# Products on zeros in TensorE's early waits, and a register list laid out in pieces of 64 bytes, in a windowed-attention and mixture-of-experts kernel

## Chip, cores, metric

One core of a Trainium2 chip. The metric is the device time of one execution in microseconds (us): the median of three runs of the kernel before is 216.32 us, from 215.83 to 216.89.

## What is computed

The input is q, k and v of 8 batches, 8 heads, 576 positions and 64 channels. Every position attends to the positions at most 32 away. The result, 4608 tokens of 512 channels, goes through a mixture of eight experts in which each token uses the one with the largest logit.

```python
scores = scale * np.matmul(q, k.transpose(0, 1, 3, 2))
mask = np.abs(pos[:, None] - pos[None, :]) <= window        # window = 32
attn = softmax(np.where(mask, scores, -1e9))
x = np.matmul(attn, v)        # as (N, D) = (4608, 512)
logits = x @ w_gate + modality_bias[modality_id]
e_idx = np.argmax(logits, axis=1)
for e in range(8):
    mask = e_idx == e
    h = np.maximum(x[mask] @ w1[e], 0.0)
    out[mask] = gate_w[mask, None] * (h @ w2[e])
```

## The kernel before

The modality bias of these inputs is large, so all tokens of one modality go to one expert. The kernel sorts the tokens by modality into one transposed list XT, with the tokens of modality 0 from the left and the others from the right, and multiplies each side by the weights of its one expert. A check of all this at the end leads to a general branch if it does not hold.

**The order is written out by hand.** The string ORDER names every piece of work in the order in which it is recorded. A piece is a name, numbers, an engine after a slash, and the PSUM banks after a colon. Each engine runs its own pieces in this order and waits where an input is not there. So a piece that waits holds back what stands behind it on its engine, and nothing on the others. The pieces that matter here:

- `l` loads q and k of a batch (line 211, issued by GpSimd), `t` transposes them on VectorE (line 651). `lv` loads v, `W` loads an expert's weights.
- `MA` and `MB` write the band mask into PSUM as products of `ident` and `neg` (lines 660, 664). `SA` and `SB` are the scores of one group of four heads (line 683), `sa` and `sb` their exponentials on ScalarE (lines 691, 694).
- `V` multiplies with v (line 725), `v` divides by the row sums on VectorE (lines 737, 738) into `xt`. `M` masks on VectorE (line 708), in all heads whose mask was not put into PSUM.
- `s` works out each token's place in the list: `s0` on ScalarE (line 163), `s1`, `s4`, `s5`, `s7` on TensorE, and `s9` writes the place of each of the 40 blocks of tokens as an integer to `off_i` (line 476 ff.).
- `r0` to `r3` load these places, ten at a time, into registers of ScalarE (line 768), which uses them as addresses in `pa` and `pb`, the copies of a block to the list (lines 779, 793). `X` makes a block's columns (line 759).
- `Je` and `Jo` make one-hot tables on VectorE and GpSimd (lines 503, 519, 522, 525), from which `Jm` (line 533) makes the list of output rows.
- `U` is the product with w1 (line 897), `u` its ReLU (line 914), `D` the product with w2 (line 923), `y` the scaling and `O` the scattered store (line 942).

A list of ten places is 40 bytes, and the four lists lie behind one another in `off_i`, so that they begin at byte 0, 40, 80 and 120:

```python
off_i = const.tile([P, NC], I32)
_, rs_ = nc.values_load_multi_w_load_instructions(
    off_i[0:1, n_ * i:n_ * i + n_], engines=[ET.Activation], min_val=0, max_val=N,
```

A piece `n` (function `idle`, line 949) exists in the code, but ORDER does not use it: it writes products that nobody reads into a bank.

Of the kernel before, what the change touches and what calls it, by code (L numbers as in the profile page):

```python
# [31 lines left out]


ORDER = """
Km Kw0/v l0.1.0/p l0.0.0/p Kp0/a Kj/p l0.1.1/p e0/v e1/v Kp1/v Kn0/p Kq1/v Kq0/v l0.0.1/p MA0.0:0123 Ke/v Kw2/v l1.0.2/p
Kh/v t0.0.1/v Ki Kw1/p Kn1/p e2/v e3/v e4/v t0.0.0/v Kg lv0.0/p Ko1/v t0.1.1/v SA0.0 Kc5/p MA0.1:4567 sa0.0/a t0.1.0/v
Kc1/p Kv/p lv0.1/p SA0.1 Kc3/p MB0.0:0123 sa0.1/a t1.1.0/v l1.1.2/p SB0.0 W1.0/p Ko0/v s0/a t1.0.0/v MB0.1:4567 sb0.0/a
SB0.1 Kc2/p sb0.1/a s1:0 Kc0/p V0:12 s2/v s3/v Kc4/p s4 s5 v0/v lv1.0/p Kb/a V2:34 s6/v s8/v s11/v e6/v V1:12 v2/v s12/p
s7 V3:56 e7/p Kc6/p v1/v s9/a s10/a r0/a W1.1/p t1.0.1/v r1/a lv1.1/p v3/v SA1.0:0123 W2.0/p s13/v t1.1.1/v SB1.0:4567
sa1.0/a l2.0.2/p s15/v Ko2/v e8/v s14/v s17/v sb1.0/a G0/v SB1.1:0123 s16/v c0/v Je1.0/v Je0.0/v Jy2/v Je0.1/p sb1.1/a  # L40
X0.0:5 M5/v X0.4:4 l2.1.2/p X0.1:7 Je0.2/p Jy10/v Jo1/v l3.1.2/p pb0.0/a X0.2:2 M4/v pa0.0/a V5:01 pb0.1/a e5/p l3.0.2/p
X0.3:5 pa0.1/a v5/v pb0.2/a Je1.1/p V4:67 pa0.2/a pb0.3/a Jo0/v Je1.2/p pa0.3/a SA1.1:0123 lv2.0/p v4/v pb0.4/a pa0.4/a
Jm0:5 G1/v sa1.1/a Kc7/p U0.1:4 Jo2/v U0.0:6 Je2.0/v u0.1/a M7/v U1.3:0 Je2.1/p Je3.0/v W2.1/p U1.0:7 M6/v u1.3/a u0.0/a
e9/p V7:12 Je3.1/v u1.0/a Je2.2/v U0.2:6 v7/v lv2.1/p V6:34 u0.2/a U0.3:0 r2/a Je3.2/p v6/v U1.2:1 Jo3/v u0.3/a L0:7
X1.2:0 X1.0:6 lo0/v Jx0/v Jm1:3 pa1.0/a X1.1:7 D0.1.0:4 Je5.0/v pb1.0/a Jx1/v Jo5/v Je5.1/p pb1.1/a D0.0.0:6 E0/a
pa1.1/a sm0/v Je4.0/v pb1.2/a rc0/v G2/v Je4.1/p X1.3:3 pa1.2/a X1.4:7 D0.0.1 pa1.3/a t2.0.0/v pa1.4/a D0.1.1 pb1.3/a
Jo4/v pb1.4/a U2.3:0 y0.1/a Je5.2/v Je4.2/v t2.0.1/v L1:3 u1.2/a Jm2:7 y0.0/a U3.2:5 lo1/v u2.3/a s19/v Jo6/v SB2.0:1234
Je7.0/v U2.2:0 Je7.1/v sb2.0/a Je7.2/v Jx2/v U2.1:6 t2.1.1/v U2.0:7 t2.1.0/v u2.1/a u2.2/a SA2.0:1234 Jo7/v u2.0/a
U3.3:6 E1/a sa2.0/a Je6.0/v U3.1:7 t3.0.1/v Je6.1/p U1.1:0 Je6.2/p u3.1/a M9/v l4.0.2/p u3.3/a SA2.1:1234 u1.1/a M8/v
lv3.0/p D2.0.0:7 sa2.1/a Jm3:0 D2.0.1 l4.1.2/p Jx3/v sm1/v u3.2/a Jy1/v lv3.1/p Jy3/v SB2.1:0123 Jy0/v Jy4/v t3.0.0/v  # L50
D2.1.0:6 sb2.1/a Jy5/v V9:45 rc1/v D2.1.1 v9/v y2.0/a V8:01 M10/v y2.1/a SB3.0:2345 U3.0:6 v8/v sb3.0/a D1.1.0:7 M11/v
V10:01 r3/a Jy8/v Jy6/v V11:45 v10/v D1.1.1 u3.0/a v11/v D1.0.0:0 y1.1/a Jy7/v X2.0:2 Jy9/v X2.1:3 G3/v X2.2:7 O0.1/p
pa2.0/a D3.1.0:1 pb2.0/a t4.1.0/v pa2.1/a X2.3:6 pb2.1/a O0.0/p D3.0.0:2 pa2.2/a t4.0.0/v pb2.2/a D1.0.1 pa2.3/a pb2.3/a
X2.4:7 D3.0.1 y1.0/v pb2.4/a pa2.4/a t3.1.1/v O1.0/p D3.1.1 SA3.0:4567 t3.1.0/v O2.0/p U5.0:0 sa3.0/a t4.1.1/v U4.2:3
y3.0/v u5.0/a SB3.1:4567 u4.2/v O3.0/p U5.2:2 sb3.1/a M12/v U4.3:3 O1.1/p M13/v U5.1:0 y3.1/a l5.1.2/p t4.0.1/v V12:45
u5.1/a O2.1/p U5.3:1 u5.2/a v12/v u4.3/a L2:0 l5.0.2/p V13:67 lo2/v SA3.1:2345 E2/a lv4.1/p v13/v U4.0:0 sa3.1/a u5.3/v
l6.1.2/p U4.1:6 u4.0/a D5.0.0:1 M14/v u4.1/a SB4.0:2345 sm2/v c1/v M15/v D4.0.0:0 sb4.0/a V14:67 c2/v rc2/v D5.0.1 v14/v
V15:23 y5.0/a c3/v SA4.1:4567 v15/v O5.0/p D4.0.1 sa4.1/a t5.1.1/v X3.0:2 D4.1.0:1 lv5.0/p pa3.0/a y4.0/v X3.1:5 pb3.0/a
X3.4:3 X3.2:6 pa3.1/a t5.1.0/v lv4.0/p D4.1.1 pb3.1/a pa3.2/a X3.3:0 t5.0.0/v pb3.2/a D5.1.0:2 pa3.3/a pb3.3/a
# [1165 lines left out]
```

## Time and profile before

| | |
|---|---|
| median of three runs | 216.32 us (215.83 to 216.89) |
| the profiled execution | 216.04 us |
| its span, first to last instruction | 214.4 us |
| mean granted TensorE clock of the span | 0.962 |
| busy: TensorE, VectorE, ScalarE, GpSimd | 189.3, 151.5, 133.8, 99.0 us |
| q, k, v and weights moved by GpSimd's DMA queue | 27.79 MB with the stores |

In the rows below PE is TensorE, PEld its weight load, DVE VectorE, ACT ScalarE, POOL GpSimd. A letter q behind an engine is its sequencer. L12 is line 12 of the kernel. Times are us from the start of the span unless marked ns.

### The profile page before, as it was taken

The numbers are of one execution on the slowest core, as the hardware profiler recorded it, in microseconds if no ns is written. First come the engines' busy times: TensorE is split into PE (matmuls) and PEld (weight loads), VectorE is DVE, ScalarE is ACT, GpSimd is POOL, SyncE is SP. The second block draws the span as 40 slices with busy tenths as digits, with TensorE's granted clock in tenths as the row PEclk, the third lists the DMA queues.
The fourth block names the chain that finished last, engine by engine and source line by source line (L and its number), as shares of the span: only waits on it lengthen the run. The fifth ranks groups of instructions, "written<-read, shape, count | busy, mean of one in ns | idle before, by whom it ended". The sixth has DMA issues, their size and how long they took to land.

```text
span 214.4 us, 6043 instructions
## 1 busy us (share of the span) xinstructions
PE 189.3 (88%) x2474; PEld 135.7 (63%) x2497; DVE 151.5 (71%) x300; ACT 133.8 (62%) x224; POOL 99.0 (46%) x138
## 2 busy tenths in 40 slices
PE   0578469999999989999999999999999999999940
PEld 0246368868766568558875786686597668566610
DVE  3865989899889896899899588977377527311610
ACT  5149397588976468697688679859974622244110
POOL 7886779950710656168640673240070322025350
PEclk9999758999999999999999999999999999999995
DMA  4999999999999349999999799224030121113211
GB/s 73 172 173 203 194 206 198 211 214 192 192 189 140 145 151 180 193 186 175 222 187 96 252 158 158 101 98 189 12 121 32 50 101 49 49 52 147 98 63 47
DMA packets 47629, 30.39 MB, mean 142 GB/s; under 512 B 38852, under 2 KB 38892, under 8 KB 47340
## 3 DMA queue, kind: packets, MB, share of 16 engines
q0 software_dynamic: 46576, 27.79, 82.0%
q1 hardware_dynamic: 1019, 2.16, 2.9%
q8 instruction: 21, 0.34, 0.7%
...
HBM read 36.76 MB, written 9.70 MB: 217 GB/s over the span
## 4 chain that ended last, share of the span: by engine, by line
PE 76%; POOL 7%; DVE 5%; DMA 3%; issue 3%; ACT 2%; another core or an unknown queue 1%; POOLq 0%; DVEq 0%
PE banks L923 29%; PE banks L897 26%; PE banks L683 7%; PE banks L725 7%; PE banks L759 3%; DMA qk<-in_q_dram 3%; POOL qk L211 2%; PE banks L824 2%; DVE qk L651 2%; ACT pt L691 1%; POOL ev L525 1%; PE banks L660 1%; DVE xt L738 1%; POOL ev L522 1%
## 5 line engine op out<-in xcount | busy, mean ns | idle before, releaser
L942 POOL DMA_INDIRECT out_dram<-ys,ids x37 | 42.0, 1136 | 91.8 <-ACT ys L933 39.9
L897 PE MATMUL banks<-XT,w_sb 128*128 128x256 bf16 x576 | 70.3, 273 | 0.3 <-DVE xt L738 0.3
L923 PE MATMUL banks<-w_sb,hT 128*128 128x512 bf16 x265 | 67.7, 379 | 1.2
L897 PEld LDWEIGHTS <-w_sb 128*128 128x128 bf16 x576 | 54.3, 98 | 11.8 <-issue 1.6
L691 ACT ACTIVATE pt<-banks 128x1536 bf16<-128x1536 f32 x32 | 46.4, 1452 | 24.3 <-PE banks L683 17.9
L914 ACT ACTIVATE hT<-banks 128x512 bf16<-128x512 f32 x56 | 31.7, 599 | 21.2 <-PE banks L897 20.8
L923 PEld LDWEIGHTS <-hT 128*128 128x128 bf16 x296 | 26.6, 98 | 24.3 <-issue 0.6
L651 DVE STREAM_TRANSPOSE qk<-qk 128x576 int32<-128x576 int32 x32 | 38.7, 1248 | 3.5 <-DMA qk<-in_q_dram 2.0
L708 DVE TENSOR_TENSOR pt<-pt,mask 128x1920 bf16<-128x1920 bf16 x28 | 32.1, 1166 | 6.1 <-ACT pt L691 4.6
L683 PE MATMUL banks<-qk 32*128 32x192 bf16 (+1 forms) x640 | 20.9, 260 | 7.2 <-DVE qk L651 3.5
L738 DVE TENSOR_TENSOR xt<-banks,recs 128x640 bf16<-128x640 f32 x32 | 26.4, 825 | 1.1
L912 DVE TENSOR_SCALAR hT<-banks 128x512 bf16<-128x512 f32 x18 | 12.4, 688 | 18.3 <-PE banks L897 18.2
L725 PE MATMUL banks<-vt,pt 128*128 128x65 bf16 x576 | 23.9, 196 | 1.6 <-ACT pt L694 1.2
L725 PEld LDWEIGHTS <-pt 128*128 128x128 bf16 x576 | 22.1, 100 | 4.2 <-issue 1.2
L683 PEld LDWEIGHTS <-qk 32*128 32x128 bf16 x640 | 14.2, 100 | 15.2 <-issue 9.6
L933 ACT ACTIVATE ys<-banks,Gt 128x512 f32<-128x512 f32 x20 | 13.6, 691 | 11.6 <-PE banks L923 11.5
L779 ACT CAST XT<-banks 128x352 f32 (+3 forms) x40 | 18.0, 451 | 3.8 <-PE banks L759 3.2
L227 POOL DMA_DIRECT2D vt<-in_v_dram x16 | 20.3, 1274 | 0.0
L793 ACT CAST XT<-banks 128x352 f32 (+2 forms) x39 | 17.6, 451 | 3.3 <-PE banks L759 2.6
L935 DVE TENSOR_SCALAR ys<-banks,Gt 128x512 f32<-128x512 f32 x17 | 12.5, 735 | 7.8 <-PE banks L923 4.9
L759 PE MATMUL banks<-oh,xt 128*128 128x128 bf16 (+1 forms) x160 | 13.1, 224 | 1.4 <-ACT pt L694 1.4
L759 PEld LDWEIGHTS <-xt 128*128 128x128 bf16 x160 | 10.7, 103 | 4.8 <-issue 1.5
...
## 6 DMA issues: line engine op xcount, KB each, us to landing
vt<-in_v_dram POOLq DMA_DIRECT2D x16, 288.0 KB
...
qk<-in_q_dram POOLq DMA_DIRECT2D x7, 576.0 KB
qk<-in_k_dram POOLq DMA_DIRECT2D x7, 576.0 KB
...
out_dram<-ys,ids POOLq DMA_INDIRECT x37
qk<-in_k_dram POOLq DMA_DIRECT2D x2, 288.0 KB
qk<-in_q_dram POOLq DMA_DIRECT2D x2, 288.0 KB
```

What stands on the lines that cost most here:

```text
L227: nc.gpsimd.dma_start(v_t[b % NV][:, n_ * i:n_ * i + n_, 0:D], v[b].rearrange("h s d -> (h s) d").rearrange("(n p) d -> p n d", p=P)[:, n_ ...
L651: nc.vector.transpose(qk_t[b % 2][:, g, at:at + S].rearrange("p (t r) -> p r t", r=R), Ct["l", b][:, u, g].bitcast(I32).rearrange("p (r j) ...
L683: nc.tensor.matmul(st[:, h, WIN * i_:WIN * i_ + w_], qk[32 * h:32 * h + 32, c_, QK + k0:QK + k0 + P], qk[32 * h:32 * h + 32, c_, q0:q0 + w ...
L691: nc.scalar.activation(pt[:, :, 2 * part:2 * part + 2, 0:WIN], st[:, :, 0:2 * WIN].rearrange("p h (j c) -> p h j c", c=WIN), ACT.Exp, scal ...
L708: nc.vector.tensor_tensor(out=p_ap, in0=p_ap, in1=mask[:], op=ALU.mult)
L725: nc.tensor.matmul(o_ap, pt[:, c1:c1 + P], vt[:, g0 + j, 0:D + 1], start=(m == 0 and i_ == 0), stop=(i_ == len(mine) - 1), skip_group_chec ...
L738: nc.vector.tensor_tensor(out=x_t[b % NX][:, :, P * hp:P * hp + P].rearrange("p m (h d) -> p h m d", h=2), in0=o_v[:, :, :, 0:D], in1=rec. ...
L759: nc.tensor.matmul(t_[:, kd, :], x_t[b % NX][:, m, P * kd:P * kd + P], Ct["oh", b][:, m, 0:n_], start=True, stop=True, skip_group_check=True)
L897: ins = nc.tensor.matmul(ph[:, u_, :], w1[:, f0:f0 + 2 * P - 1:2], rhs, start=(kd == 0), stop=(kd == n_kd - 1))
L914: nc.scalar.activation(o_ap, i_ap, ACT.Relu)
L923: nc.tensor.matmul(Ct["D", t_, s_], Ct["h", t_][:, kf, P * s_:P * s_ + P], w2, start=(kf == 0), stop=(kf == n_kf - 1))
L942: ins = nc.gpsimd.indirect_dma_start(out=out, out_offset=bass.IndirectOffsetOnAxis(ap=ids[:, u_:u_ + 1], axis=0), in_=Ct["y", t_, s_][:], ...
```

## The change

ORDER gets 24 pieces `n`, of four or two products of 256 columns each, 64 products in all. Their weights and their data are `zero_b`, a tile of zeros (the weights were `ident` in the unused function). Some names of other pieces change places in the string, but on every engine the other instructions stand in the order in which they stood. `off_i` gets 16 places for each list of ten, so that the lists begin at byte 0, 64, 128 and 192.

```diff
 ORDER = """
-Km Kw0/v l0.1.0/p l0.0.0/p Kp0/a Kj/p l0.1.1/p e0/v e1/v Kp1/v Kn0/p Kq1/v Kq0/v l0.0.1/p MA0.0:0123 Ke/v Kw2/v l1.0.2/p
+Km Kw0/v n4.256:0 l0.1.0/p l0.0.0/p n4.256:0 Kp0/a Kj/p n4.256:0 l0.1.1/p e0/v e1/v n4.256:0 Kp1/v Kn0/p Kq1/v n4.256:0
...
-    off_i = const.tile([P, NC], I32)
+    off_i = const.tile([P, B // RB, 16], I32)
...
-            copy(eng, off_i[:], Ct["off"][:, 0:NC])
+            copy(eng, off_i[:, :, 0:RB * NM], Ct["off"][:, 0:NC].rearrange("p (a c) -> p a c", c=RB * NM))
...
-            off_i[0:1, n_ * i:n_ * i + n_], engines=[ET.Activation], min_val=0, max_val=N,
+            off_i[0:1, i, 0:n_], engines=[ET.Activation], min_val=0, max_val=N,
...
-            nc.tensor.matmul(banks[:, bk[0], 0:w_], ident[:], zero_b[:, 0:w_], start=True, stop=True, skip_group_check=True)
+            nc.tensor.matmul(banks[:, bk[0], 0:w_], zero_b[:, 0:P], zero_b[:, 0:w_], start=True, stop=True, skip_group_check=True)
```

**First place: TensorE from its first instruction to the first scores.** Before, the mask products MA0.0 come first and the scores SA0.0 right behind them:

```order
L660 LDWEIGHTS ident [waits Pool_49]
L660 MATMUL banks<-neg,ident 128x384 [waits Pool_49]
...
L660 LDWEIGHTS ident
L660 MATMUL banks<-neg,ident 128x384
L683 LDWEIGHTS qk_84 [waits DVE_49]
L683 MATMUL banks<-qk_84 128x192 [waits DVE_49]
```

Now 28 products on zeros stand ahead of MA0.0, and 18 between MA0.0 and SA0.0:

```order
L953 LDWEIGHTS zero_b [waits DVE_49]
L953 MATMUL banks<-zero_b 128x256
...
L662 LDWEIGHTS ident [waits Pool_49]
L662 MATMUL banks<-neg,ident 128x384 [waits Pool_49]
...
L953 LDWEIGHTS zero_b
L953 MATMUL banks<-zero_b 128x256
...
L685 LDWEIGHTS qk_84 [waits DVE_49]
L685 MATMUL banks<-qk_84 128x192 [waits DVE_49]
```

The first of them wait for VectorE's memset of `zero_b` alone; the scores still wait for VectorE's transposes.

**Second place: TensorE behind SB0.1**, where the transpose s1 (line 459, now 461), the products V0, s4 and s5 (lines 467 and 470, now 469 and 472) and V2 follow. Before:

```order
L459 LDWEIGHTS midr [waits Activation_49]
L459 MATMUL banks<-ident,midr 128x40 [waits Activation_49]
L725 LDWEIGHTS pt_86 [waits DMASW5_49]
...
L467 LDWEIGHTS Am [waits DVE_49]
L467 MATMUL banks<-ones,Am 40x128
L470 LDWEIGHTS tri [waits Pool_49]
```

Now:

```order
L953 LDWEIGHTS zero_b
L953 MATMUL banks<-zero_b 128x256 [waits Activation_49]
...
L461 LDWEIGHTS midr
L461 MATMUL banks<-ident,midr 128x40
L727 LDWEIGHTS pt_86 [waits DMASW5_49]
...
L472 LDWEIGHTS tri [waits Pool_49]
L472 MATMUL banks<-Am,tri 128x40
L953 LDWEIGHTS zero_b
L953 MATMUL banks<-zero_b 128x256
...
L727 MATMUL banks<-vt_88,pt_87 128x65 [waits DMASW6_49]
```

Two products stand ahead of s1 and carry its wait for ScalarE's sb0.0 (both use bank 0); six stand between s5 and V2.

**Third place: TensorE between V3 and SA1.0.** Before, the scores of batch 1 followed V3 at once. Now ten products stand there, which wait first for VectorE (v2, bank 3) and then for ScalarE (s9 and s10, bank 0):

```order
L727 MATMUL banks<-vt_88,pt_87 128x65
L953 LDWEIGHTS zero_b
L953 MATMUL banks<-zero_b 128x256
...
L953 MATMUL banks<-zero_b 128x256 [waits DVE_49]
...
L953 MATMUL banks<-zero_b 128x256 [waits Activation_49]
...
L685 LDWEIGHTS qk_85 [waits DVE_49]
L685 MATMUL banks<-qk_85 128x192
```

Nothing on the other engines waits for a product on zeros, and behind SA1.0 TensorE's order has none.

## Rows read from the trace of the kernel before

**Rows 1.** Busy time in stretches; columns as in the first line

```profile
core 0: us, PE busy (x) PEld busy (x) DVE busy (x) ACT busy (x) POOL busy (x), PEclk, DMA share, GB/s
0.00:17.08 17.08, 8.51 (x77) 4.36 (x78) 10.36 (x32) 7.12 (x7) 13.86 (x45) 1.00 1.20 141
17.08:23.91 6.83, 4.25 (x105) 3.44 (x103) 5.09 (x14) 4.75 (x9) 4.34 (x12) 1.00 1.16 212
23.91:34.15 10.24, 7.58 (x136) 6.63 (x136) 8.93 (x23) 8.46 (x15) 8.32 (x11) 0.50 1.60 192
41.50:205.00 163.50, 160.85 (x2060) 114.66 (x2082) 119.30 (x217) 108.34 (x187) 63.65 (x60) 1.00 0.79 137
```

**Rows 2.** Chain that ended last, 12 to 21 us: start, us, what

```profile
12.23 0.83 PE banks L683 x15
13.06 1.39 PE banks L660 x4
14.45 0.43 PE banks L664 x4
14.88 0.97 PE banks L683 x24
...
17.23 0.22 PE banks L664 x4
17.45 0.60 PE banks L683 x20
...
18.07 1.45 ACT pt L691
19.52 0.49 ACT pt L694
...
20.07 0.53 PE banks L725 x11
```

**Rows 3.** Timeline of VectorE: start, us, engine, line, what, idle before

```profile
1.04 0.17 DVE L316 MEMSET zero_b<- 128x128 uint32 x1 [1.04 <-PEq L1209]
...
13.96 2.50 DVE L651 STREAM_TRANSPOSE qk<-qk 128x576 int32<-128x576 int32 x2 [1.78 <-DMA qk<-in_q_dram]
...
22.67 1.25 DVE L651 STREAM_TRANSPOSE qk<-qk 128x576 int32<-128x576 int32 x1
```

**Rows 4.** Timeline of TensorE: first scores, first product with w1

```profile
8.87 0.83 PE L683 MATMUL banks<-qk 32*128 32x192 bf16 x16 [2.39 <-DVE qk L651]
...
34.73 1.47 PE L897 MATMUL banks<-XT,w_sb 128*128 128x256 bf16 x12
```

**Rows 5.** Timeline of ScalarE

```profile
14.46 0.29 ACT L163 CAST midr<-mid 40x128 bf16<-40x128 int32 x1
...
21.78 0.19 ACT L163 CAST off_i<-banks 128x40 int32<-128x40 f32 x1
...
25.58 2.79 ACT L691 ACTIVATE pt<-banks 128x1536 bf16<-128x1536 f32 x2 [3.52 <-DVE posi L487]
...
34.45 1.45 ACT L691 ACTIVATE pt<-banks 128x1536 bf16<-128x1536 f32 x1 [0.19 <-PE banks L683]
```

**Rows 6.** Register loads, line 768: ns min/median/max; r0, r1, then r2 with r3

```profile
L768 ACTq TENSOR_LOAD <-off_i x1: 1193/1193/1193, 22.0 to 22.0; - x1
L768 ACTq TENSOR_LOAD <-off_i x1: 2173/2173/2173, 23.3 to 23.3; - x1
L768 ACTq TENSOR_LOAD <-off_i x2: 997/1596/2194, 39.9 to 63.7; - x2
```

**Rows 7.** The page's DMA issues: what, engine, count, KB each

```profile
vt<-in_v_dram POOLq DMA_DIRECT2D x16, 288.0 KB
...
qk<-in_k_dram POOLq DMA_DIRECT2D x7, 576.0 KB
```

**Rows 8.** Timeline of GpSimd

```profile
29.14 1.87 POOL L525 TENSOR_SCALAR ev<-ev,pr 128x180 bf16<-128x180 bf16 x1
...
33.56 0.96 POOL L525 TENSOR_SCALAR ev<-ev,pr 128x180 bf16<-128x180 bf16 x1
```

More of the change, by code (lines that the diff above doesn't have):

```diff
@@ L34 @@
 ORDER = """
-Km Kw0/v l0.1.0/p l0.0.0/p Kp0/a Kj/p l0.1.1/p e0/v e1/v Kp1/v Kn0/p Kq1/v Kq0/v l0.0.1/p MA0.0:0123 Ke/v Kw2/v l1.0.2/p
[L36 to L54, printed above, removed]
@@ L55 @@
-y3.0/v u5.0/a SB3.1:4567 u4.2/v O3.0/p U5.2:2 sb3.1/a M12/v U4.3:3 O1.1/p M13/v U5.1:0 y3.1/a l5.1.2/p t4.0.1/v V12:45
-u5.1/a O2.1/p U5.3:1 u5.2/a v12/v u4.3/a L2:0 l5.0.2/p V13:67 lo2/v SA3.1:2345 E2/a lv4.1/p v13/v U4.0:0 sa3.1/a u5.3/v
+Km Kw0/v n4.256:0 l0.1.0/p l0.0.0/p n4.256:0 Kp0/a Kj/p n4.256:0 l0.1.1/p e0/v e1/v n4.256:0 Kp1/v Kn0/p Kq1/v n4.256:0
+Kq0/v l0.0.1/p Ke/v n4.256:0 Kw2/v l1.0.2/p Kh/v t0.0.1/v Ki n4.256:0 Kw1/p Kn1/p MA0.0:0123 e2/v e3/v n4.256:4 e4/v
+t0.0.0/v n2.256:4 Kg n2.256:4 n2.256:4 lv0.0/p n2.256:4 Ko1/v n2.256:4 t0.1.1/v n2.256:4 n2.256:4 SA0.0 Kc5/p MA0.1:4567
@@ new lines @@
+sa0.0/a t0.1.0/v Kc1/p Kv/p lv0.1/p SA0.1 MB0.0:0123 Kc3/p sa0.1/a t1.1.0/v SB0.0 l1.1.2/p s0/a W1.0/p Ko0/v t1.0.0/v
+MB0.1:4567 sb0.0/a Kc2/p SB0.1 Kc0/p n2.256:0 s1:0 sb0.1/a V0:12 Kc4/p s2/v s3/v s4 s5 n2.256:3 v0/v n2.256:3 lv1.0/p
+n2.256:3 s6/v Kb/a s8/v V2:34 s11/v e6/v s12/p V1:12 e7/p v2/v Kc6/p s7 V3:56 n2.256:7 v1/v W1.1/p n2.256:3 s9/a s10/a
+n2.256:4 r0/a n2.256:0 n2.256:0 t1.0.1/v lv1.1/p r1/a v3/v SA1.0:0123 W2.0/p s13/v sa1.0/a t1.1.1/v SB1.0:4567 l2.0.2/p
+s15/v Ko2/v sb1.0/a e8/v SB1.1:0123 s14/v s17/v G0/v s16/v c0/v Je1.0/v Je0.0/v sb1.1/a X0.0:5 Jy2/v M5/v Je0.1/p X0.4:4
@@ new lines @@
+X0.1:7 l2.1.2/p Jy10/v Jo1/v Je0.2/p pb0.0/a X0.2:2 pa0.0/a l3.1.2/p M4/v V5:01 pb0.1/a pa0.1/a e5/p l3.0.2/p pb0.2/a
+X0.3:5 pa0.2/a v5/v V4:67 Je1.1/p pb0.3/a pa0.3/a Je1.2/p Jo0/v pb0.4/a SA1.1:0123 lv2.0/p pa0.4/a v4/v Jm0:5 sa1.1/a
+U0.1:4 G1/v Kc7/p Jo2/v U0.0:6 u0.1/a Je2.0/v U1.3:0 M7/v Je2.1/p U1.0:7 Je3.0/v u1.3/a W2.1/p M6/v u0.0/a V7:12 e9/p
+u1.0/a U0.2:6 Je3.1/v Je2.2/v v7/v lv2.1/p V6:34 u0.2/a U0.3:0 r2/a v6/v Je3.2/p U1.2:1 u0.3/a Jo3/v L0:7 X1.2:0 X1.0:6
+lo0/v Jx0/v Jm1:3 pa1.0/a X1.1:7 D0.1.0:4 Je5.0/v pb1.0/a Jx1/v Jo5/v Je5.1/p pb1.1/a D0.0.0:6 E0/a pa1.1/a sm0/v
@@ new lines @@
+Je4.0/v pb1.2/a rc0/v G2/v Je4.1/p X1.3:3 pa1.2/a X1.4:7 D0.0.1 pa1.3/a t2.0.0/v pa1.4/a D0.1.1 pb1.3/a Jo4/v pb1.4/a
+U2.3:0 y0.1/a Je5.2/v Je4.2/v t2.0.1/v L1:3 u1.2/a Jm2:7 y0.0/a U3.2:5 lo1/v u2.3/a s19/v Jo6/v SB2.0:1234 Je7.0/v
+U2.2:0 Je7.1/v sb2.0/a Je7.2/v Jx2/v U2.1:6 t2.1.1/v U2.0:7 t2.1.0/v u2.1/a u2.2/a SA2.0:1234 Jo7/v u2.0/a U3.3:6 E1/a
+sa2.0/a Je6.0/v U3.1:7 t3.0.1/v Je6.1/p U1.1:0 Je6.2/p u3.1/a M9/v l4.0.2/p u3.3/a SA2.1:1234 u1.1/a M8/v lv3.0/p
+D2.0.0:7 sa2.1/a Jm3:0 D2.0.1 l4.1.2/p Jx3/v sm1/v u3.2/a Jy1/v lv3.1/p Jy3/v SB2.1:0123 Jy0/v Jy4/v t3.0.0/v D2.1.0:6
@@ new lines @@
+sb2.1/a Jy5/v V9:45 rc1/v D2.1.1 v9/v y2.0/a V8:01 M10/v y2.1/a SB3.0:2345 U3.0:6 v8/v sb3.0/a D1.1.0:7 M11/v V10:01
+r3/a Jy8/v Jy6/v V11:45 v10/v D1.1.1 u3.0/a v11/v D1.0.0:0 y1.1/a Jy7/v X2.0:2 Jy9/v X2.1:3 G3/v X2.2:7 O0.1/p pa2.0/a
+D3.1.0:1 pb2.0/a t4.1.0/v pa2.1/a X2.3:6 pb2.1/a O0.0/p D3.0.0:2 pa2.2/a t4.0.0/v pb2.2/a D1.0.1 pa2.3/a pb2.3/a X2.4:7
+D3.0.1 y1.0/v pb2.4/a pa2.4/a t3.1.1/v O1.0/p D3.1.1 SA3.0:4567 t3.1.0/v O2.0/p U5.0:0 sa3.0/a t4.1.1/v U4.2:3 y3.0/v
+u5.0/a SB3.1:4567 u4.2/v O3.0/p U5.2:2 sb3.1/a M12/v U4.3:3 O1.1/p M13/v U5.1:0 y3.1/a l5.1.2/p t4.0.1/v V12:45 u5.1/a
@@ L57 @@
+O2.1/p U5.3:1 u5.2/a v12/v u4.3/a L2:0 l5.0.2/p V13:67 lo2/v SA3.1:2345 E2/a lv4.1/p v13/v U4.0:0 sa3.1/a u5.3/v
 l6.1.2/p U4.1:6 u4.0/a D5.0.0:1 M14/v u4.1/a SB4.0:2345 sm2/v c1/v M15/v D4.0.0:0 sb4.0/a V14:67 c2/v rc2/v D5.0.1 v14/v
```

## The prediction

> **What bounds the kernel now.** I read the stretches first. From 41.5 us to 205 us TensorE is busy for 160.85 of 163.50 us [rows 1], and it runs one fixed order of work. So the end moves by as much as TensorE's first product with w1 (U0.1, at 34.73 us [rows 4]) moves, as long as the data come in time. Everything this change can win or lose lies ahead of that point. There the granted clock has a dip: 0.50, the lower of the two levels, from 23.91 to 34.15 us [rows 1]. The 1.00 of the first stretch is not a reading: the record of the clock begins at 17.08, and the products tell what went on before. Four products of 128 columns took 0.43 us of the chain at 14.45 and 0.22 us at 17.23 [rows 2]. [...]
>
> The chain that ended last then tells where the lower clock costs time: from 12.23 to 18.07 us it is all TensorE [rows 2]. From 18.07 on it is ScalarE and VectorE, and later GpSimd's tables, and a product of half the length changes little there.
>
> **The products on zeros, first place.** Weights and data are there when VectorE's memset ends, at 1.04 + 0.17 = 1.21 us [rows 3]. Four products of 384 columns take 1.39 us at the lower level [rows 2], so one of 256 takes 1.39 / 4 x 256 / 384 = 0.23 us, and 0.12 us at the upper. No row shows a product of zeros, so their effect on the clock is bounded from both sides: none (a rival below), or that of any other product. I take the second. The nearest row is the mask product, which is nearly all zeros too, and the clock rose at 17.08 behind a stretch half made of those. Then 28 products run from 1.2 to 7.7 us at the most, and the clock rises during them or soon after. MA0.0 follows (0.7 us at the upper level) and 18 more (2.2 us), so the scores SA0.0 start near 10 us instead of 8.87 [rows 4]. That costs nothing: the next scores, SA0.1, start at 12.23 [rows 2] because VectorE's transpose ends then, and SA0.0 with the mask MA0.1 needs only 0.83 + 1.39 = 2.2 us even at the lower level. The cover is gone once SA0.0 starts after 10.0 at the lower level or 11.1 at the upper.
>
> **The chain from 12.23.** SA0.1 falls from 0.83 to some 0.45 us (20 products took 0.60 at the upper level [rows 2]), so ScalarE's sa0.1 starts 0.4 us earlier, at 12.7. Behind it TensorE needs half of 1.39, 0.43 and 0.97 for the mask and SB0.0, which is 1.4 us, about ScalarE's 1.45. So from here ScalarE is the bound and runs without a wait: sa0.1 1.45, s0 0.29 [rows 5], sb0.0 1.45 and 0.49. Then sb0.1 starts at 12.7 + 3.7 = 16.4 instead of 18.07 [rows 2]: **1.7 us earlier**. That is less than the 2.5 us by which TensorE's own pieces shrink.
>
> **Second and third place.** Two products ahead of s1 cost 0.2 us, six ahead of V2 0.7. V2's last eleven products wait for ScalarE's sb0.1 anyway, to 20.07 before [rows 2], now to 18.4, and the eight products, s1, V0, s4, s5 and V2's first part (some 2.1 us behind sb0.0's end at 16.4) reach 18.5. So 0.1 us is lost, and 1.6 us is kept. The ten products behind V3 (1.2 us) lie in TensorE's wait for VectorE's next transpose. They wait for VectorE and ScalarE themselves, but only for work that ends over a microsecond before that transpose does.
>
> **The transpose at 22.67** [rows 3] then could start at 21.0. It needs k of batch 1. The load before it had landed at 13.96, since VectorE waited for it until then [rows 3]; behind it the queue carries two halves of v and then this k, 2 x 288 + 576 = 1152 KB, 1.18 MB [rows 7]. At 141 to 212 GB/s [rows 1] that takes 8.4 to 5.6 us, so it lands between 19.5 and 22.3. I take 21.2, a rate a little under that of the stretch from 17.08: **1.5 us earlier**. The data would be the next bound.
>
> **The lists of 64 bytes.** The loads of r0 and r2 took 1.19 and 1.00 us, those of r1 and r3 2.17 and 2.19 [rows 6]. All load ten numbers. The two long ones lie at bytes 40 to 79 and 120 to 159, across a multiple of 64; the short ones do not. So r1 and r3 should lose some 1.1 us each. r3 is loaded beside other work of ScalarE and gives nothing. r1 counts: before it stands off_i (21.78), behind it ScalarE's sa1.0 (25.58) [rows 5], and off_i comes 1.7 us earlier. With the shorter r1 ScalarE is free at 25.58 - 1.7 - 1.1 = 22.8. The scores SA1.0 end at 21.2 + 1.25 + 0.5 = 23.0. So sa1.0 starts **2.6 us earlier**. From there to 34.45 ScalarE hardly waits: of its 1.78 idle us in the dip (10.24 less 8.46 [rows 1]), 1.67 lie between 23.91 and 25.58 [rows 1, 5]. So it keeps this lead.
>
> [...]
>
> **Up to U0.1.** U0.1 stands behind Jm0, which needs GpSimd's table of 33.56 + 0.96 = 34.52 [rows 8]. GpSimd starts on its tables when VectorE gets there, 1.5 us earlier. Its first piece on line 525 took 1.87 us, the second, on as much data, 0.96 [rows 8]; the long one ran beside VectorE's product with the mask. That product waits for ScalarE, whose lead is larger by 1.1 us, so the two should overlap less. If all 0.9 us go, U0.1 is 2.4 us earlier; if none, 1.5. I take 2.3.
>
> **The dip.** After SA1.0 no product on zeros stands. TensorE's work from there to some 28 us is as thin as before, so I expect the clock to fall about where it fell, and to return when TensorE has no more gaps. If it does not return before 34.15, U0.1 and what follows run up to 1.8 us at half rate, which costs 0.9. I charge 0.2.
>
> **Sum.** 2.3 - 0.2 = 2.1 us, on the profiled execution's 216.04: 213.9 us. The median stood 0.28 above it, which gives **214.2 us**. The loads behind k of batch 1 are needed 2 us earlier too. How early they land the rows don't show. All waits of TensorE from 41.5 us on sum to 2.65 us [rows 1], so none came much too late before, and I cost them at nothing; a load that came just in time would give some of the lead back, and the range has room for that.
>
> **Rivals.**
> - *The clock falls again between 10.8 and 12.2 us* (0.15). TensorE waits for the transpose there, with no products put in. In its favour, the clock fell at 23.91 behind a stretch in which TensorE worked 4.25 of 6.83 us [rows 1]. Then the chain from 13 us runs as before, and only SA0.1's 0.4 us and a bit of r1 are left: 215.7 us.
> - *GpSimd holds everything* (0.15): the 1.87 us piece stays, U0.1 gains 1.5 and pays 0.2 for the dip: 215.0 us.
> [...]
> - *No dip, and GpSimd's table early* (0.05): 2.9 us gained: 213.4 us.
> - *Slower: zeros don't raise the clock* (0.07). Then the change does not do what its part on TensorE says. The 46 products take 46 x 0.23 = 10.6 us, MA0.0 1.39, and SA0.0 starts at 13.2. SA0.1 follows 0.83 + 1.39 later, at 15.4, 3.2 us after its time. It decides from 10.0 us on, where the cover above ends. Half a microsecond comes back in later waits: 216.3 + 2.7 = 219.0 us. Against it speaks the rise at 17.08.
>
> **Chances and range.** The forecast has 0.50. What a measurement here can tell from no change is 0.5%, 1.1 us, so faster means under 215.2 and slower over 217.4. Faster: forecast, most of GpSimd's case and of r1's, the early case, a little of the clock's, 0.73. Same: 0.18. Slower: 0.09, the zeros and a little for a wait that I overlooked. The range takes in the early case with the spread of the runs (213.0) and the case of the clock (up to 216.3); the slower case is left out.
>
> **What would show it.** Right: SA0.0 near 10 us, the granted clock's record beginning before 9 us, and 0.5 us or less for SA0.1; sb0.1 near 16.4; the transpose near 21.2; r1 and r3 near 1.1 us; sa1.0 near 23.0; U0.1 near 32.4. Wrong: a record of the clock that begins after 12, a fall of it between 10 and 17, a load of r1 near 2 us, a wait of VectorE for k beyond 22, or new gaps of TensorE after 41.5 that give the lead back.

## The result

The changed kernel takes 214.02 us (median of six runs, 213.62 to 214.76), the kernel before beside it 216.17 us (215.56 to 216.89). The ratio is 0.9904, with a 95% interval from 0.9882 to 0.9926. The forecast was 214.2 us. The profiled execution took 213.69 us; the sum had given 213.9.

### The profile after

The lines of the code stand two lower than before, because ORDER is two lines longer (L685 was L683, L899 was L897). The stretches of the changed kernel, cut where the granted clock changes; the rows before are [rows 1]:

```profile
core 0: us, PE busy (x) PEld busy (x) DVE busy (x) ACT busy (x) POOL busy (x), PEclk, DMA share, GB/s
1.20:4.53 3.33, 3.27 (x16) 2.34 (x17) 0.89 (x4) 2.58 (x3) 2.90 (x7) 1.00 0.55 72
4.53:12.20 7.67, 5.43 (x56) 4.06 (x55) 6.78 (x26) 1.45 (x1) 6.93 (x21) 1.00 1.07 183
12.20:25.01 12.81, 10.43 (x238) 8.06 (x237) 10.19 (x26) 9.37 (x13) 10.38 (x27) 1.00 1.55 191
25.01:31.84 6.83, 5.13 (x86) 4.45 (x76) 6.70 (x14) 6.60 (x14) 5.30 (x8) 0.50 1.48 197
41.50:203.00 161.50, 158.85 (x2017) 112.54 (x2037) 117.54 (x212) 107.39 (x185) 63.00 (x57) 1.00 0.80 139
```

The record of the clock now begins at 4.53 us, not at 17.08. As before, the 1.00 of the stretch ahead of the record is no reading: there 15 or 16 products took 3.27 us, 0.20 to 0.22 us each, which is the lower of the two levels (at the upper, ten took 1.25 us, at 20.20 below). From 4.53 to 25.01 the granted clock is 1.00. The dip is still there, 0.50 from 25.01 to 31.84. From 41.5 us on TensorE's waits sum to 161.50 - 158.85 = 2.65 us, just as before [rows 1]: nothing was given back later.

TensorE's timeline shows the three places; x is the number of products, and the brackets give the idle time ahead and what ended it:

```profile
1.26 4.81 PE L953 MATMUL banks<-zero_b 128*128 128x256 bf16 x28 [1.26 <-DVE zero_b L318]
...
6.55 2.13 PE L953 MATMUL banks<-zero_b 128*128 128x256 bf16 x18
8.84 0.53 PE L685 MATMUL banks<-qk 32*128 32x192 bf16 x16 [0.16 <-DVE qk L653]
...
12.21 0.53 PE L685 MATMUL banks<-qk 32*128 32x192 bf16 x16 [2.08 <-DVE qk L653]
...
16.37 0.38 PE L953 MATMUL banks<-zero_b 128*128 128x256 bf16 x2 [0.48 <-ACT pt L696]
...
17.66 0.81 PE L953 MATMUL banks<-zero_b 128*128 128x256 bf16 x6
...
20.20 1.25 PE L953 MATMUL banks<-zero_b 128*128 128x256 bf16 x10
22.42 0.60 PE L685 MATMUL banks<-qk 32*128 32x192 bf16 x17 [0.97 <-DVE recs L739]
...
32.27 3.66 PE L899 MATMUL banks<-XT,w_sb 128*128 128x256 bf16 x32
```

SA0.0 is on time (8.84; it was 8.87 [rows 4]), SA0.1 takes 0.53 us for 0.83 [rows 2], and U0.1 starts at 32.27 instead of 34.73 [rows 4]. ScalarE's timeline, against [rows 2, 5]:

```profile
12.78 1.45 ACT L693 ACTIVATE pt<-banks 128x1536 bf16<-128x1536 f32 x1 [1.91 <-PE banks L685]
14.18 0.31 ACT L165 CAST midr<-mid 40x128 bf16<-40x128 int32 x1
...
16.22 1.43 ACT L693 ACTIVATE pt<-banks 128x1536 bf16<-128x1536 f32 x1
...
19.90 0.18 ACT L165 CAST off_i<-banks 128x40 int32<-128x40 f32 x1
...
23.04 2.79 ACT L693 ACTIVATE pt<-banks 128x1536 bf16<-128x1536 f32 x2 [2.87 <-PE banks L685]
```

From 12.78 on (sa0.1) ScalarE runs without a wait through sb0.1 (16.22) to off_i (19.90). Then it loads registers, and sa1.0 (23.04) waits for TensorE's scores and no longer for the load. The four loads, in ns (min/median/max), first and last start in us:

```profile
L770 ACTq TENSOR_LOAD <-off_i x4: 987/1000/1202, 20.1 to 61.2; - x4
```

None is long; before, two of the four took 2173 and 2194 ns [rows 6]. The chain that ended last has new pieces:

```profile
7.43 6.66 DMA mid<-in_moe_modality_id_dram
...
14.18 0.31 ACT midr L165
...
21.20 1.16 DVE qk L653
...
27.58 1.20 POOL ev L527
...
31.18 0.87 POOL ev L527
...
34.70 1.15 POOL slk L393
35.85 0.07 issue
35.92 1.15 POOL slk L394
```

It begins with a load: the modality ids that s0 reads land at 7.43 + 6.66 = 14.09 us, just as ScalarE gets to s0. Then come VectorE's transpose and GpSimd's tables, whose long piece is down from 1.87 [rows 8] to 1.20 us. In VectorE's timeline the transpose follows the product ahead of it without a wait for data:

```profile
20.38 0.82 DVE L740 TENSOR_TENSOR xt<-banks,recs 128x640 bf16<-128x640 f32 x1
21.12 1.25 DVE L653 STREAM_TRANSPOSE qk<-qk 128x576 int32<-128x576 int32 x1
```

Between 12 and 18 us no piece of TensorE of more than 0.4 us is left on the chain but V0.

### The profile page after: what moved, and what is told of

It is laid out like the page before. It is cut to its first block, busy times and chain, and to the rows that moved or that the text cites. A ratio compares the mean times of both kernels' runs of the same rounds, so it can differ in the third digit from the quotient of the medians.

```text
span 212.0 us, 6172 instructions
## 1 busy us (share of the span) xinstructions
PE 193.3 (91%) x2538; PEld 140.2 (66%) x2561; DVE 151.8 (72%) x300; ACT 133.5 (63%) x224; POOL 99.3 (47%) x138
## 3 DMA queue, kind: packets, MB, share of 16 engines
q1 hardware_dynamic: 1019, 2.16, 3.0%
## 4 chain that ended last, share of the span: by engine, by line
PE 48%; issue 16%; POOL 15%; DMA 9%; DVE 6%; ACT 2%; SPq 1%; POOLq 0%; ACTq 0%
PE banks L925 20%; PE banks L899 18%; POOL out_dram L944 5%; DMA qk<-in_k_dram 4%; PE banks L727 4%; POOL vt L229 3%; DMA mid<-in_moe_modality_id_dram 3%; PE banks L685 2%; POOL qk L213 2%; PE banks L761 2%; DVE xt L740 2%; DMA mb_bc<-n_moe_modality_bias_dram 1%; PE banks L826 1%; DVE qk L653 1%; POOL ev L527 1%
## 5 line engine op out<-in xcount | busy, mean ns | idle before, releaser
L944 POOL DMA_INDIRECT out_dram<-ys,ids x37 | 43.3, 1170 | 90.8 <-ACT ys L935 39.4
L899 PE MATMUL banks<-XT,w_sb 128*128 128x256 bf16 x576 | 70.3, 273 | 0.3 <-DVE xt L740 0.3
L899 PEld LDWEIGHTS <-w_sb 128*128 128x128 bf16 x576 | 54.4, 98 | 11.7 <-issue 1.6
L685 PE MATMUL banks<-qk 32*128 32x192 bf16 (+1 forms) x640 | 19.0, 242 | 4.6 <-DVE qk L653 2.9
L685 PEld LDWEIGHTS <-qk 32*128 32x128 bf16 x640 | 12.6, 93 | 11.7 <-issue 7.9
```

The costliest lines, as they stand in the source:

```text
L685: nc.tensor.matmul(st[:, h, WIN * i_:WIN * i_ + w_], qk[32 * h:32 * h + 32, c_, QK + k0:QK + k0 + P], qk[32 * h:32 * h + 32, c_, q0:q0 + w ...
L899: ins = nc.tensor.matmul(ph[:, u_, :], w1[:, f0:f0 + 2 * P - 1:2], rhs, start=(kd == 0), stop=(kd == n_kd - 1))
L944: ins = nc.gpsimd.indirect_dma_start(out=out, out_offset=bass.IndirectOffsetOnAxis(ap=ids[:, u_:u_ + 1], axis=0), in_=Ct["y", t_, s_][:], ...
```

## Experiments

The chips differ: the kernel before takes 214.26 to 214.57 us on two of the three used below, and 216.0 on the other. So each ratio is taken against runs of the kernel before on the same chip. Starts are in us, from the profiled execution of each kernel. The second line of the table is the execution shown above. In the edits below, long lines of ORDER are cut to the part that changes.

| kernel | ratio, 95% interval | sb0.1 | sa1.0 | U0.1 | granted clock |
|---|---|---|---|---|---|
| before | 1 | 18.07 | 25.58 | 34.73 | up 17.08, down 23.91 to 34.15 |
| changed | 0.9904 [0.9882, 0.9926] | 16.22 | 23.04 | 32.27 | up 4.53, down 25.01 to 31.84 |
| lists alone | 0.9961 [0.9942, 0.9979] | 18.48 | 25.01 | 34.49 | up 17.96, down 24.78 to 35.02 |
| zeros alone | 0.9949 [0.9929, 0.9970] | 16.39 | 23.86 | 33.30 | up 6.63, down 27.11 to 33.94 |
| lists, first 46 products | 0.9892 [0.9866, 0.9919] | 16.13 | 23.05 | 32.27 | up 4.11, down 24.59 to 31.41 |
| lists, later 18 products | 0.9958 [0.9941, 0.9974] | 17.68 | 24.51 | 33.74 | up 15.45, down 25.68 to 32.51 |
| lists, first 28 products | 0.9947 [0.9923, 0.9971] | 17.50 | 24.02 | 33.25 | up 5.22, down 12.05 to 15.46, 25.70 to 32.53 |
| 28 more products ahead of SA0.0 | 0.9982 [0.9956, 1.0008] | 18.16 | 24.99 | 34.22 | up 6.45, down 26.93 to 33.75 |
| 8 more in the later waits | 0.9920 [0.9890, 0.9950] | 16.17 | 23.05 | 32.48 | up 6.67, down 27.15 to 33.98 |
| lists moved by 28 bytes | one run | 16.04 | 25.07 | 34.12 | up 4.54, down 25.02 to 31.84 |
| lists 48 bytes apart | one run | 17.70 | 24.53 | 33.76 | up 5.36, down 12.19 to 15.60, 25.84 to 32.67 |
| ident as weights | 0.9931 [0.9906, 0.9955] | 16.25 | 23.20 | 32.63 | up 6.53, down 27.00 to 33.83 |
| the wait at 10 to 12 us filled | 0.9917 [0.9903, 0.9931] | 16.19 | 23.10 | 32.47 | up 5.08, down 25.56 to 32.39 |
| changed, again | 0.9923 [0.9899, 0.9947] | 16.16 | 23.49 | 32.71 | up 5.03, down 25.51 to 32.34 |

### Which part brings what

**Lists alone.** The kernel before with the new layout:

```diff
-    off_i = const.tile([P, NC], I32)
+    off_i = const.tile([P, B // RB, 16], I32)
...
-            off_i[0:1, n_ * i:n_ * i + n_], engines=[ET.Activation], min_val=0, max_val=N,
+            off_i[0:1, i, 0:n_], engines=[ET.Activation], min_val=0, max_val=N,
```

> The kernel before with the lists in pieces of 64 bytes and no products on zeros. My theory (the load of r1 is on the path, but TensorE's clock holds most of it): r1 and r3 load in about 1.0 us instead of 2.17; ScalarE is then free at 24.4, the scores SA1.0 end near 24.8, so sa1.0 starts some 0.8 us earlier than 25.58; GpSimd's tables keep part of that, and U0.1 gains 0.3 to 0.8 us: 215.6 us (215.3 to 215.9), ratio about 0.997. Rival A, the list does most of the change's work: 214.6 us or less. [...]

All four loads took 986 to 1183 ns. The median fell from 214.54 to 213.71 us, 0.8 us, a little more than the 0.6 expected. In ScalarE's timeline of this kernel:

```profile
18.48 1.45 ACT L691 ACTIVATE pt<-banks 128x1536 bf16<-128x1536 f32 x1 [0.55 <-PE banks L683]
...
25.01 2.84 ACT L691 ACTIVATE pt<-banks 128x1536 bf16<-128x1536 f32 x2 [2.53 <-PE banks L683]
```

From sb0.1 to sa1.0 it is 25.01 - 18.48 = 6.53 us, against 25.58 - 18.07 = 7.51 before: 1.0 us less, though the profiled execution (214.86 us) was the longest of its twelve, with a clock that rose 0.9 us later and a U0.1 that gained only 0.24 us. sa1.0 now waits for TensorE, as expected. Rival A falls.

**Zeros alone.** The changed kernel with the old layout:

```diff
-    off_i = const.tile([P, B // RB, 16], I32)
+    off_i = const.tile([P, NC], I32)
...
-            off_i[0:1, i, 0:n_], engines=[ET.Activation], min_val=0, max_val=N,
+            off_i[0:1, n_ * i:n_ * i + n_], engines=[ET.Activation], min_val=0, max_val=N,
```

> The changed kernel with the old list of 40 places. My theory: the clock rises near 4.5 us as in the changed kernel, sb0.1 starts at 16.2 and the transpose at 21.1, but r1 takes 2.17 us again, so that sa1.0 starts near 24.2 instead of 23.0; VectorE's and GpSimd's lead covers half of that, U0.1 comes 0.6 us later than in the changed kernel: 214.6 us (214.3 to 215.2). Rival A, the list does most: 215.5 or more. Rival C, the list adds nothing once the clock is up: 214.0, the changed kernel's time.

Up to sa1.0 the places are as expected: sb0.1 at 16.39, sa1.0 at 23.86, and r1 long again. What I expected behind it failed: sa1.0 is 0.82 us later than in the changed kernel and U0.1 1.03, not 0.6, so VectorE and GpSimd covered nothing of it. The gain is smaller than the middle of what was expected, 0.51% or 1.1 us, and inside its range (214.3 to 215.2 on 216.17 is 0.991 to 0.996). The end of the dip lay behind the start of U0.1 here; the price of that comes up below. 1.1 and 0.8 us together are 1.9, close to the 2.1 of the whole. So each brings roughly half, and neither needs the other; the two intervals overlap, so which brings more is not shown.

**The first 46 products or the later 18.** The changed kernel without one or the other group. For the first of the two the edit is

```diff
-Kc2/p SB0.1 Kc0/p n2.256:0 s1:0
+Kc2/p SB0.1 Kc0/p s1:0
...
-r0/a n2.256:0 n2.256:0 t1.0.1/v
+r0/a t1.0.1/v
```

> The changed kernel with the first 46 products on zeros only; the 18 in the second and third place are left out. My theory (the rise of the clock before 12 us is all that the zeros bring): the clock rises near 4.5 us as before; without the second place V2 and s1 come 0.1 to 0.2 us earlier; the clock falls one reading earlier or where it fell (18 to 25 us). If it falls at 18 to 20, SA1.0 costs 0.4 us more and the time is 214.4; if not, 213.9. Between: 214.1 us (213.8 to 214.6). Rival D, the later products are needed to hold the clock through ScalarE's chain: it falls before 16 us and the time is 215.2 or more.

> The changed kernel with only the 18 products in the second and third place; the first 46 are left out, and the aligned lists stay. My theory: the clock rises at 17.08 as in the kernel before or a little earlier, the chain from 12 to 17 us runs at half rate, and what is left is the list's gain less some 0.2 us for products at half rate ahead of s1 and V2: 215.7 us (215.3 to 216.2). Rival D, the later products do the work: 214.5 or less. Rival E: the products of the second place, 0.23 us each at the lower level, delay V2 and cost more than the list brings: 216.4 or more.

The first 46 alone give all of it (0.9892, U0.1 at 32.27), the later 18 alone no more than the lists do without them (0.9958 against 0.9961). So the products of the second and third place neither hold the clock (up from 4.11 to 24.59 without them, from 4.53 to 25.01 with them) nor cost anything that can be measured. What they delayed is hidden by data: without them the chain of that kernel runs through the load of v of batch 0, which V2 waits for until 18.28.

```profile
11.12 7.17 DMA vt<-in_v_dram
18.28 0.04 issue
18.32 0.73 PE banks L727 x18
```

### What the head must do

**Only 28 products.** Without the 18 between MA0.0 and SA0.0, and without the later 18, so that the run with the first 46 alone is the one to compare:

```diff
-Kn1/p MA0.0:0123 e2/v e3/v n4.256:4 e4/v
+Kn1/p MA0.0:0123 e2/v e3/v e4/v
...
-t0.0.0/v n2.256:4 Kg n2.256:4 n2.256:4 lv0.0/p n2.256:4 Ko1/v n2.256:4 t0.1.1/v n2.256:4 n2.256:4 SA0.0
+t0.0.0/v Kg lv0.0/p Ko1/v t0.1.1/v SA0.0
```

> Only the first 28 products on zeros; the 18 between MA0.0 and SA0.0 and the 18 later ones are left out; the lists stay aligned. TensorE then idles some 2.2 us between MA0.0's end (6.6) and SA0.0 (8.84), and 2 us more before 12.2. My theory (the clock follows what TensorE did shortly before, so the 18 products carry it across the wait): it rises near 4.5 us and falls before 13; the mask and the scores from 12.2 run at half rate again, sb0.1 starts near 17.8 and U0.1 near 33.8: ratio 0.995 to 0.997, as with the later products alone. Rival F, once risen the clock lasts to 20 us or more whatever lies between: sb0.1 near 16.2, U0.1 at 32.3, ratio 0.989 to 0.991.

The clock rose and fell again before the chain from 12 us. The stretches of this kernel:

```profile
5.22:12.05 6.83, 3.15 (x39) 1.99 (x40) 6.09 (x20) 1.45 (x1) 6.16 (x19) 1.00 1.08 182
12.05:15.46 3.41, 3.41 (x48) 2.12 (x47) 1.44 (x3) 1.65 (x2) 2.71 (x9) 0.50 1.99 158
15.46:25.70 10.24, 6.44 (x164) 4.83 (x160) 8.45 (x24) 7.49 (x11) 7.64 (x19) 1.00 1.44 199
```

In the first of them TensorE worked 3.15 of 6.83 us at the upper level, then came 3.41 us at the lower one, in which ScalarE had to wait for the scores. The ratio, 0.9947, is just under the expected 0.995 to 0.997; the first 46 gave 0.9892. This is the prediction's first rival, brought about on purpose.

**A head that is too long.** Seven pieces of two products became seven of six:

```diff
-t0.0.0/v n2.256:4 Kg n2.256:4 n2.256:4
+t0.0.0/v n6.256:4 Kg n6.256:4 n6.256:4
```

> The changed kernel with 46 products instead of 18 between MA0.0 and SA0.0. My theory of the cover: 28 more products at 0.118 us end near 12.0 us instead of 8.68, beyond the 11.1 us at which the cover is gone; SA0.0 with the mask MA0.1 then takes 1.2 us, SA0.1 starts near 13.2 instead of 12.21, and ScalarE's sb0.1 comes 1.0 to 1.3 us later, at 17.2 to 17.5; the transpose and U0.1 follow by 0.8 to 1.2 us (U0.1 near 33.3): ratio 0.994 to 0.996. Rival G, there is still slack behind SA0.1 (the data of batch 1 land at 21 us anyway): U0.1 stays at 32.3 to 32.6 and the ratio at 0.989 to 0.991.

The cover ends where the prediction had put it, but behind it each microsecond costs more than I had expected. SA0.0 starts at 12.61 here, because the clock also rose later, at 6.45. ScalarE's timeline:

```profile
13.18 2.79 ACT L693 ACTIVATE pt<-banks 128x1536 bf16<-128x1536 f32 x2 [9.38 <-PE banks L685]
15.86 0.30 ACT L165 CAST midr<-mid 40x128 bf16<-40x128 int32 x1
16.33 1.45 ACT L693 ACTIVATE pt<-banks 128x1536 bf16<-128x1536 f32 x1 [0.18 <-PE banks L685]
...
18.16 1.46 ACT L693 ACTIVATE pt<-banks 128x1536 bf16<-128x1536 f32 x1
```

sa0.0 and sa0.1 now run one behind the other, where sa0.0 used to be done before 12 us; I had left that out. sb0.1 is 18.16 - 16.22 = 1.94 us later and U0.1 34.22 - 32.27 = 1.95: nothing ahead of U0.1 takes any of the delay up. The ratio, 0.9982, lies above the expected 0.994 to 0.996. Rival G falls.

### What the dip costs

Eight more products in the later waits of the changed kernel:

```diff
-r0/a n2.256:0 n2.256:0 t1.0.1/v
+r0/a n2.256:0 n8.256:0 t1.0.1/v
...
-t1.1.1/v SB1.0:4567
+t1.1.1/v n2.256:4 SB1.0:4567
```

> The changed kernel with eight more products in TensorE's later waits: six more (0.7 us) in the wait of 0.97 us before SA1.0 and two (0.24 us) in the 0.28 us before SB1.0. Every other wait up to 28 us lies where all eight banks hold live data, so nothing can be put there. My theory (the dip costs next to nothing, because GpSimd's table and ScalarE's copies set U0.1): whether the fall at 25 us comes later or not at all, U0.1 stays within 0.2 us of 32.27 and the ratio at 0.989 to 0.991. Rival H, the dip still costs half a microsecond or more: with the clock held through 28 us U0.1 comes at 31.8 or before and the ratio falls to 0.987 or less. If the clock falls at 25 us anyway, the run tells only that the eight products are free.

The eight products cost nothing that can be seen (0.9920, and sa1.0 at 23.05), but the clock falls all the same, at 27.15. It fell as late without them where it had risen as late (zeros alone, 27.11; ident, 27.00), so they have no part in that. What the run does show is a price of the dip. In TensorE's timeline the clock comes back at 33.98, after U0.1 has begun:

```profile
32.48 4.39 PE L899 MATMUL banks<-XT,w_sb 128*128 128x256 bf16 x32
```

The same 32 products took 3.66 us in the kernel before and where the dip ends before U0.1 (the changed kernel, 31.84; first 46 products, 31.41). U0.1 also starts 0.21 us later than in the changed kernel, with sa1.0 in the same place: Jm0 ahead of it took 0.78 us instead of 0.54. So a dip that lasts into U0.1 costs up to 0.9 us there, according to when the clock rose. That a dip which ends before U0.1 costs nothing is argued, since the chain of the changed kernel has no piece of TensorE between 17.54 and 39.06 us. No run shows it, because all of them have the dip; rival H is untested.

### Which lists load fast

**Moved by 28 bytes.** The old layout in the changed kernel, seven places further on:

```diff
-    off_i = const.tile([P, B // RB, 16], I32)
+    off_i = const.tile([P, NC + 8], I32)
...
-            off_i[0:1, i, 0:n_], engines=[ET.Activation], min_val=0, max_val=N,
+            off_i[0:1, n_ * i + 7:n_ * i + n_ + 7], engines=[ET.Activation], min_val=0, max_val=N,
```

> The changed kernel with the old layout, forty places behind one another, but moved by 28 bytes: the lists lie at bytes 28 to 67, 68 to 107, 108 to 147 and 148 to 187. My theory (a load that crosses a multiple of 64 bytes takes about twice as long, and where in the 64 bytes it lies doesn't matter): now r0 and r2 take about 2.2 us, although only one number of r0 lies beyond the border, and r1 and r3, which crossed before, take about 1.0. Rival I (a list must begin at a multiple of 64): all four take about 2.2. Rival J (r1 and r3 were long for what runs beside them, not for their place): r1 and r3 stay at 2.2 and r0 and r2 at 1.0 to 1.2.

All four loads are long, also that of r1, which now lies in one piece of 64 bytes (68 to 107):

```profile
L770 ACTq TENSOR_LOAD <-off_i x4: 2178/2184/2367, 20.3 to 62.9; - x4
```

So my theory fell. It is not the border of 64 bytes. Two long loads in a row make sa1.0 25.07 - 23.04 = 2.03 us later, with the clock rising and falling at the same times, and the one run took 216.36 us, as much as the kernel before (216.0).

The lists that loaded in 1.0 to 1.2 us began at bytes 0 and 80, and at 0, 64, 128 and 192; those that took 2.2 us at 40 and 120, and at 28, 68, 108 and 148. The first are the multiples of 16.

**48 bytes apart.** Twelve places a list, so that r1 and r2 lie across a border of 64:

```diff
-    off_i = const.tile([P, B // RB, 16], I32)
+    off_i = const.tile([P, B // RB, 12], I32)
```

> The changed kernel with 12 places a list instead of 16: the lists begin at bytes 0, 48, 96 and 144, so that those of r1 and r2 lie across a multiple of 64. My theory after the shifted layout (what counts is whether a list begins at a multiple of 16 bytes; 0 and 80 were short, 40, 120, 28, 68, 108 and 148 long): all four take about 1.0 us, r0 1.2. Rival (a list must lie in one piece of 64 bytes, as the prediction has it, and the shifted layout has another reason): r1 and r2 take about 2.2. Rival (a list must begin at a multiple of 32): r1 and r3 take about 2.2.

```profile
L770 ACTq TENSOR_LOAD <-off_i x4: 994/998/1193, 21.6 to 62.7; - x4
```

All four are short, also those of r1 and r2 (1001 and 994 ns), which cross a border of 64. In these runs every list that began at a multiple of 16 bytes, counted from the start of `off_i`, loaded at some 100 ns a register (998 / 10; the first of a kernel at 118 to 120), and every other at 217 to 219 (2184 / 10; the first at 237).

This run had a second result. All 64 products are in it, and still the clock fell in the wait before 12.2 us:

```profile
1.20:5.36 4.16, 4.10 (x20) 2.94 (x21) 1.72 (x11) 2.58 (x3) 3.66 (x9) 1.00 0.64 95
5.36:12.19 6.83, 4.95 (x52) 3.61 (x51) 6.03 (x19) 1.45 (x1) 6.16 (x19) 1.00 1.10 186
12.19:15.60 3.41, 3.33 (x48) 2.12 (x47) 1.81 (x4) 1.64 (x2) 2.71 (x9) 0.50 2.06 156
```

U0.1 came at 33.76, 1.5 us later than in the profile above, and this one run took 214.43 us where the kernel before takes 214.57. The prediction's first rival is thus not false but comes in some executions: in one of the eight profiled here that had the whole head of 46 products and nothing put into the wait (the longer head aside).

### The start, and the wait that was left open

**ident as weights.** The 28 first products stand directly ahead of MA0.0, and all 64 have the weights that the function had before:

```diff
-            nc.tensor.matmul(banks[:, bk[0], 0:w_], zero_b[:, 0:P], zero_b[:, 0:w_], start=True, stop=True, skip_group_check=True)
+            nc.tensor.matmul(banks[:, bk[0], 0:w_], ident[:], zero_b[:, 0:w_], start=True, stop=True, skip_group_check=True)
```

> The changed kernel with ident as the weights of the products on zeros, as in the unused function before; the data stay zeros. My theory: the first product waits for GpSimd's ident, which ends at 3.4 us, so 28 products start at 3.4 instead of 1.26, the clock rises 2 us later, near 6.5 to 7, and the last of the 46 ends near 11.0 to 11.4, right at the point where the cover of SA0.0 ends: U0.1 at 32.3 to 32.8, ratio 0.990 to 0.993. Rival (zero weights count for less, and real weights raise the clock sooner): the record begins within 2 us of the first product and the end is at 10.2 or before. Rival (the start has no slack): ratio 0.995 or more.

```profile
3.42 4.73 PE L952 MATMUL banks<-zero_b,ident 128*128 128x256 bf16 x28 [3.42 <-POOL ident masks.py:199]
...
10.70 0.52 PE L684 MATMUL banks<-qk 32*128 32x192 bf16 x16
...
12.21 0.53 PE L684 MATMUL banks<-qk 32*128 32x192 bf16 x16 [0.23 <-DVE qk L652]
```

The start is 2.16 us later, as expected, and the rise (6.53) comes 3.1 us after the first product. With zero weights it came 2.9 to 5.4 us after it (4.11 to 6.67 after 1.26), so no advantage of real weights is seen. SA0.0 starts at 10.70, still inside the cover, and SA0.1 on time. 0.9931 is just over the expected 0.990 to 0.993; U0.1's 32.63 is inside its range, though here the dip lies across U0.1.

**The wait filled.** Eight products between MA0.1 and SA0.1 of the changed kernel:

```diff
-Kc1/p Kv/p lv0.1/p SA0.1
+Kc1/p Kv/p lv0.1/p n8.256:0 SA0.1
```

> The changed kernel with eight more products on zeros between MA0.1 and SA0.1. They write bank 0, so they wait until ScalarE's sa0.0 has read it (10.9 us) and end near 11.9, before the transpose that SA0.1 waits for ends at 12.2: TensorE's wait of 2.0 us there falls into two of 0.8 and 0.3. Theory (the clock can fall in that wait, and did in one of the seven profiled executions that held the first 46 products with data of SA0.0 on time): with the wait broken up the clock stays at its upper level from its rise to 24 us or later, U0.1 comes at 32.2 to 32.7, the slowest executions of the changed kernel go, and the median gains 0 to 0.4 us: ratio 0.987 to 0.990, and no run more than 1 us above the fastest. Rival (the fall there is chance and rare, or the products are in the way): ratio 0.990 to 0.993, SA0.1 no earlier, or later where sa0.0 is late.

> The changed kernel itself once more, on the same chip as the one with the wait filled, to compare the two and for a second profiled execution. Theory: ratio 0.988 to 0.993 again; the clock rises between 4 and 7 us, depending on when its record is renewed, and in most executions it lasts from there to 25 to 27 us, so that U0.1 comes at 32.2 to 32.7; if it falls in the wait before 12.2, sb0.1 starts near 17.7 and U0.1 near 33.7. Rival (0.9904 was one chip's luck): 0.995 or more.

```profile
10.99 1.03 PE L953 MATMUL banks<-zero_b 128*128 128x256 bf16 x8 [0.79 <-ACT pt L693]
12.23 0.53 PE L685 MATMUL banks<-qk 32*128 32x192 bf16 x16 [0.21 <-DVE qk L653]
```

The products lie where they were meant to lie and delay nothing. The six runs span 0.53 us (212.16 to 212.69), those of the unchanged one 1.53 us (211.99 to 213.52). An end of the executions with the fall would look like this, but the one of them that was profiled speaks against it. The unchanged kernel's slowest run, 213.52, is its profiled one, and there the clock stayed up from 5.03 to 25.51:

```profile
12.21 0.52 PE L685 MATMUL banks<-qk 32*128 32x192 bf16 x16 [2.00 <-DVE qk L653]
```

What it lost lies later: U0.1 starts 0.24 us later than with the wait filled, and from 41.5 to 200 us TensorE waits for 158.50 - 157.55 = 0.95 us, against 158.50 - 158.47 = 0.03 there. So the spread is not shown to come from the fall. The two ratios, 0.9917 and 0.9923, lie within each other's intervals, and the first missed its expected 0.987 to 0.990. The second measurement of the changed kernel, 0.9923, agrees with the first. So no version is shown to be faster than the changed kernel; the first 46 products with lists at multiples of 64 bytes do the same with less.

## Why the prediction was right

- **Zeros raise the clock.** Right; the record begins at 4.53, ahead of the forecast's 9 us. The rise comes between 4.11 and 6.67 us in the ten profiled kernels whose head begins at 1.26. "SA0.0 near 10" was too late: it starts at 8.84 in the profile above, and at 9.66 where the clock rose last and the head is as long. I had let all 28 products run at the lower level. Nothing hangs on it inside the cover, as the prediction said.
- **The chain from 12.23.** Right by its steps: SA0.1 to 0.53 us (forecast 0.45), ScalarE as the bound without a wait, sb0.1 at 16.22 (16.4). s0 lies at the same time just behind its load (14.09), a limit that the forecast had not seen.
- **Second and third place.** Costed at 0.1 us; without them U0.1 came no earlier.
- **The transpose** at 21.12 (21.2). That it came so close is in part luck. The forecast let it wait for k of batch 1 until 21.2, but VectorE ran into it without a wait, so the 21.0 of the forecast's own chain is what held; when k landed is not shown, only that it was there by 21.12. The rate behind the 21.2 was also misread: 1.18 MB in 21.2 - 13.96 = 7.24 us is 163 GB/s, well under the 212 of the stretch from 17.08 [rows 1]. The data that did bind were v of batch 0, which the forecast had not looked at: in the repeated run of the changed kernel TensorE waited 0.33 us for it at 18.76, and the transpose came at 21.56.
- **The lists.** The size was right: r1 and r3 lost 1.17 and 1.20 us. The reason was wrong: "across a multiple of 64" is refuted by the layout moved by 28 bytes and by the one of 48. It was luck that the layout worked: a multiple of 64 is also one of 16. No run shows a load of r1 that stays long with the lists at multiples of 64, the case of r1 in the chances: there the four took 0.99 to 1.20 us. With r1 long in the old layout (zeros alone, 2.17 us) nothing of sa1.0's 0.82 us was covered on the way to U0.1, where that run's expectation had let half of it be covered.
- **sa1.0** at 23.04 (23.0), **GpSimd's piece** 1.20 us (between its two ends of 0.96 and 1.87), **U0.1** at 32.27 (32.4).
- **The dip.** Charged 0.2; it ended before U0.1 in the profiled execution, where no cost is seen, and cost up to 0.9 us at U0.1 in others.
- **The sum.** 2.1 us forecast on the profiled execution, 216.04 - 213.69 = 2.35 measured; 2.15 between the medians. U0.1 gained 2.46, where 2.3 was forecast. That the medians agree to 0.1 us is luck in part: single executions of the changed kernel lie 1.1 us apart.
- **The rivals.** The fall of the clock before 12.2 was seen once with the full head, and its price was that of the forecast: 1.5 us, between 214.2 and 215.7 there, between U0.1 at 32.27 and at 33.76 here. The slower case did not come, since zeros do raise the clock, but its mechanism is real: past the cover, ScalarE's sa0.0 adds itself, and what sb0.1 loses (1.94 us) reaches U0.1 in full (1.95).
